# Logits three steps ahead of the weighted sums, the exponential one step behind its input, and masked places written by memsets

## The chip, the cores and the metric

The kernel runs on one core of a Trainium2 chip. The core has a matmul engine (PE, with PEld for the loading of weights), three engines for elementwise work (DVE, ACT and POOL) and SP, which here only issues DMAs. ACT issues some DMAs too. Each engine works through its own queue of instructions in order. An instruction waits for what it needs, and everything behind it on that engine waits with it. The metric is the device time of one execution in microseconds; of several runs the median is given.

## The reference

The input x has 2048 rows of 512 numbers. Each row is normalised, and the result xn goes two ways: into an attention over a sliding, dilated window (path A), and into a gated MLP with a product over all rows (path B).

```python
xn = _layernorm(x)
# A: H = 32 heads of Dh = 16, W = 8 taps at a distance of dil = 2 rows
q, k, v = split(xn @ wqkv)
idx = pos[:, None] - off[None, :]          # pos - 0, 2, .. 14
logits = einsum("bhsd,bhswd->bhsw", q, k[idx]) * Dh ** -0.5
logits = where(idx >= 0, logits, -1e9)
s = einsum("bhsw,bhswd->bhsd", softmax(logits), v[idx]) @ wo
# B
z = gelu(xn @ w_in)                        # 512 -> 2 * 896
z1, z2 = z[..., :896], layernorm(z[..., 896:])
g = w_sp @ z2 + b_sp                       # 2048 x 2048 by 2048 x 896
out = x + s * silu((z1 * g) @ w_out)
```

Masked are only the first 14 rows of the sequence, for which a tap would lie before row 0.

## The kernel before, in words

**PE's work.** All large products are done in float32 by three products each: a weight and its partner are split into a high and a low part, and high by high, high by low and low by high are added up in a PSUM bank. The high part is a copy on ACT (L186), the low part a subtraction on DVE (L187), both from a raw tile that a DMA has brought in (L163, four raw buffers). Every weight that PE uses thus passes through SP, ACT and DVE. PE's program in order: the products for q, k and v (L374 to L376), z1 (L640 to L660), z2 (L670 to L735), the product over rows with w_sp (L764: first block rows c = 2 and 3, into banks called g; then block products by a scheme with fewer products, into banks called p and q, whose weights are sums of blocks of w_sp, kept in sums_d, and whose partners are sums of blocks of z2, kept in t_d), w_out (L979 to L981) and wo.

**z2.** A tile z2_j of 128 rows stands in two banks, z2_j_0 with 512 columns and z2_j_1 with 384. Gelu on ACT reads each into the SBUF tile zt_j (L678), and the bank is then free for another product; the last four z2 banks become four of the banks g. Statistics are made on DVE (L687, aggregated by L688), a reciprocal root on POOL (L689 to L692), the normalisation on ACT (L696), then the split into BIG (L186, L187). Sums of two tiles' parts (L709, DVE) are stored to t_d from ACT's queue (L715).

**Attention.** q, k and v are written to DRAM (qkv_d) and read back by units: 8 groups of heads by two halves of the 16 rows that each of the 128 partitions holds, 16 units in all, and each unit in two steps of NJ = 4 rows. A partition holds 16 consecutive rows of the sequence, so the 14 masked ones are all on partition 0. For a step, the scores (L521) multiply eight shifted rows of k by q, the heads (L528) sum over 16 columns into lg. When a unit has all its logits, `shifted` adds the mask (L542), takes the maximum (L546), subtracts it (L547) and lets ACT take the exponential (L550). Then `normed` divides by the sum (L555, L556, L557), `weighted` multiplies v by lg (L563), a first fold (L573) adds four taps to four on POOL (for the last steps on DVE), and `finish` folds on (L578, L579), transposes (L586) and stores (L589, to o_d). Each of k, q, v, pr and pv has one buffer, lg has two. The loads of k and q (L501, L502) and of v (L510) are issued by SP.

**What sets the order.** Except for the exponential, the first fold and the DMAs, attention's instructions are chained in the order in which they are written (`line`). All of attention has a low priority (the heads a high one), and a scheduler weaves this chain into the work that feeds PE, on each engine's queue, ahead of the run, by its own costs. The program that comes out is fixed. Moving attention's steps against each other therefore also moves what stands between them on DVE, ACT, POOL and SP.

Of the kernel before, what the change touches and what calls it, by code (L numbers as in the profile page):

```python
# [11 lines left out]
F32 = mybir.dt.float32  # L12
F32R = mybir.dt.float32r
AF = mybir.ActivationFunctionType
ALU = mybir.AluOpType
AX = mybir.AxisListType

P = 128
# [3 lines left out]
H, DH, W, DIL = 32, 16, 8, 2  # L22
NT = S // P
# [11 lines left out]
CS = D // NSUB  # L35
Q = 32
HS = CS // DH
NBLK = GC // CS
HALO = (W - 1) * DIL
NJ = 4  # L40
PAD = 16
NH = NT // 2
# [3 lines left out]
MASKED = -1e9 * float(DH) ** 0.5  # L46
# [6 lines left out]
NOSYNC = mybir.DependencyInfo(mybir.DependencyClass.NoSync, mybir.DependencyReason.DATA)  # L53
# [4 lines left out]
def kernel(  # L58
# [13 lines left out]
    nc = tc.nc  # L72
# [14 lines left out]
    const = ctx.enter_context(tc.tile_pool(name="const", bufs=1, side="right"))  # L87
    opened = tc.tile_pool(name="tmp", bufs=1, side="right")
    tmp = opened.__enter__()
# [19 lines left out]
    nc.vector.memset(mvx, 0.0)  # L109
    mvz = const.tile([P, NT, 2], F32, name="mvz")  # L110
    nmz = const.tile([P, NT], F32, name="nmz")
    mask = const.tile([P, W, NT], F32, name="mask")

    BIG = whole.tile([P, NT * 2 * FH + 32], F32R, name="BIG")[:, 32:]

# [260 lines left out]
            nc.tensor.matmul(pq, xl[:, k], wh, start=False, stop=k == KB - 1)  # L376
        return pq

    zpad = const.tile([PAD, CS], F32, name="zpad")
    nc.vector.memset(zpad, 0.0)  # L380
    nc.vector.memset(mask, 0.0)
    for w in range(1, W):
        nc.vector.memset(mask[0:1, W - 1 - w, : DIL * w], MASKED)

    def weights(g, raw=[None] * KB):
        return [prep(wqkv[:, g, k, :], GC, f"wqkv_{g}_{k}", raw=raw[k]) for k in range(KB)]
# [91 lines left out]
    ap_ = ctx.enter_context(tc.tile_pool(name="att", bufs=1))  # L478

    def attention():  # L480
        saved = tc.cur_priority
        tc.cur_priority = LOW
        units = [(sub, h) for sub in range(NSUB) for h in range(2)]
        qs, ks, vs, lgs = {}, {}, {}, {}
        last = []

        def line(ins):
            if last:
                tc.add_manual_dep(ins.ins, last[-1].ins.name, NOSYNC, reason="attention in order")
            last.append(ins)  # L490
            return ins
# [26 lines left out]
        def scores(u, j0):  # L518
            pr = ap_.tile([P, W, NJ * CS], F32, tag="pr", name=f"pr_{u}_{j0}")
            qb = qs[u][:, j0 : j0 + NJ, :].rearrange("p j c -> p (j c)")  # L520
            line(nc.vector.tensor_tensor(  # L521
                pr, taps(ks[u], j0), qb.unsqueeze(1).to_broadcast([P, W, NJ * CS]), op=ALU.mult
            ))
            return pr

        def heads(u, j0, pr):
            tc.cur_priority = 0
            line(nc.vector.tensor_reduce(  # L528
                lgs[u][:, :, j0 * HS : (j0 + NJ) * HS],
                pr.rearrange("p w (i d) -> p w i d", d=DH),  # L530
                axis=AX.X,
                op=ALU.add,
            ))
            tc.cur_priority = LOW

        def shifted(u):
            sub, h = units[u]
            n = NH * HS
            lg = lgs[u]
            lgv = lg.rearrange("p w (j h) -> p w j h", h=HS)  # L540
            mk = mask[:, :, h * NH : (h + 1) * NH]
            line(nc.vector.tensor_tensor(  # L542
                lgv, lgv, mk.unsqueeze(3).to_broadcast([P, W, NH, HS]), op=ALU.add
            ))
            mx = ap_.tile([P, n], F32, tag="mx", name=f"mx_{u}")
            line(nc.vector.tensor_reduce(mx, lg.rearrange("p w i -> p i w"), axis=AX.X, op=ALU.max))  # L546
            line(nc.vector.tensor_tensor(  # L547
                lg, lg, mx.unsqueeze(1).to_broadcast([P, W, n]), op=ALU.subtract
            ))
            nc.scalar.activation(lg, lg, AF.Exp, scale=float(DH) ** -0.5)  # L550

        def normed(u):
            n, lg = NH * HS, lgs[u]
# [17 lines left out]
        def first_fold(part, eng):  # L571
            pv = part[2]
            eng.tensor_tensor(pv[:, 0:4], pv[:, 0:4], pv[:, 4:8], op=ALU.add)  # L573
# [18 lines left out]

        def start(u):
            load_qk(u)
            lgs[u] = ap_.tile([P, W, NH * HS], F32, tag="lg", name=f"lg_{u}", bufs=2)

        steps = [(u, j0) for u in range(len(units)) for j0 in range(0, NH, NJ)]
        ahead = NH // NJ
        start(0)
        for j0 in range(0, NH, NJ):  # L600
            heads(0, j0, scores(0, j0))
        shifted(0)
        part = None
        for i, (u, j0) in enumerate(steps):
            coming = steps[i + ahead] if i + ahead < len(steps) else None
            if coming:
                if not coming[1]:
                    start(coming[0])
                pr = scores(*coming)
            if part:  # L610
                finish(part)
            if not j0:
                load_v(u)
                normed(u)
            part = weighted(u, j0)
            if coming:
                heads(*coming, pr)
            first_fold(part, nc.gpsimd if coming else nc.vector)
            if coming and coming[1] + NJ == NH:
                shifted(coming[0])  # L620
        finish(part)
# [164 lines left out]
    for c in (2, 3):  # L786
        for n, js in enumerate(order):
            w = spatial.get((c, js)) or spatial_block(c, js)
# [122 lines left out]
    with urgent(400):  # L911
        for f in range(3):
# [5 lines left out]
        steps=([], [T2[0]], [T2[1]], [T2[2]]),  # L918
# [4 lines left out]
        steps=(  # L923
            [T2[3], later(upper_first, 0)],
            [T3[0], later(upper_first, 2)],
            [T3[1], later(late, 2, 0, 2)],
            [T3[2], later(late, 2, 2, 2)],
        ),
# [87 lines left out]
    for i in range(0, NT, 2):  # L1016
        j0 = rows_of[i]
# [67 lines left out]
```

## Time and profile before

| | |
|---|---|
| median of 3 runs | 720.46 us (719.02 to 720.86) |
| the profiled execution | 719.89 us, its span 718.1 us |
| PE busy | 704.5 us, 98% |
| DVE busy | 591.3 us, 82% |
| ACT busy | 266.2 us, 37% |
| POOL busy | 114.5 us, 16% |
| mean granted clock of PE | 0.995 |

An engine's busy time is time in which one of its instructions runs. In the timelines, a row gives the start in us from the span's start, the duration, engine, line, operation and out<-in (names without their buffer's number), and in brackets how long the engine had been idle before it and what ended the wait. In the list of waits the numbers are the total in us, how many waits, and the longest. In the table by stretches each row is a stretch, its length, and then busy time (and instructions) of PE, PEld, DVE, ACT and POOL, the granted clock, the share of the DMA engines and GB/s. The lines of the changed kernel are numbered a little differently (L186 and L187 stay near, L678 becomes L681, L696 becomes L699, L951 becomes L954).

### The profile page before, as it was taken

What the parts mean: (1) busy time and instruction counts of PE and PEld (TensorE: products, weight loads), DVE (VectorE), ACT (ScalarE), POOL (GpSimd) and SP (SyncE); (2) the same over time, 40 slices, a digit from 0 to 9 for tenths busy, and PEclk for the clock granted to TensorE, in tenths of its full rate; (3) what the DMA queues carried; (4) which work ended last, traced back from release to release, by engine and by line L of the source; (5) the groups of instructions that cost most, each with busy time, mean ns of one, the idle gap of its engine ahead of it and who ended that gap; (6) DMA issues with size and microseconds to landing.
All of it is one profiled execution on the core that took longest, in us unless ns stands there. A gap on an engine that the chain in (4) does not pass through costs nothing.

```text
span 718.1 us, 9084 instructions
## 1 busy us (share of the span) xinstructions
PE 704.5 (98%) x3152; PEld 587.3 (82%) x3152; DVE 591.3 (82%) x788; ACT 266.2 (37%) x417; POOL 114.5 (16%) x111
## 2 busy tenths in 40 slices
PE   8999999999999999799999999999998999999998
PEld 7888888888888899688888888888886888888886
DVE  6773579998999899999899999899999999330374
ACT  4343332333334566751213111325455443141520
POOL 3100011221121545421021121120110110000000
PEclk9999999999999999999999999999999999999999
DMA  8777677685987224289977843868778483264685
GB/s 281 242 198 221 181 259 215 206 244 208 332 284 260 87 73 147 98 269 342 362 238 251 293 150 108 286 208 303 248 250 294 129 285 133 103 190 176 234 285 199
DMA packets 100110, 159.29 MB, mean 222 GB/s; under 512 B 9056, under 2 KB 51296, under 8 KB 100064
## 3 DMA queue, kind: packets, MB, share of 16 engines
q1 hardware_dynamic: 61424, 116.11, 49.6%
q10 hardware_dynamic: 38640, 42.60, 17.2%
q8 instruction: 24, 0.39, 0.2%
q14 instruction: 22, 0.18, 0.1%
HBM read 107.74 MB, written 50.94 MB: 221 GB/s over the span
## 4 chain that ended last, share of the span: by engine, by line
PE 55%; DVE 21%; DMA 13%; issue 6%; ACT 2%; POOL 2%; SPq 1%; DVEq 0%; ACTq 0%
PE g L764 21%; PE q L764 5%; PE b L980 4%; PE b L979 4%; PE b L981 4%; DVE lg L528 3%; PE p L764 3%; DMA sb<-in_w_sp 3%; DVE pr L521 3%; DVE pv L563 3%; PE qkv L374 2%; PE qkv L376 2%; PE qkv L375 2%; PE s L980 2%; PE s L979 2%
## 5 line engine op out<-in xcount | busy, mean ns | idle before, releaser
L573 POOL TENSOR_TENSOR pv<-pv 128x1024 f32<-128x1024 f32 x30 | 72.2, 2407 | 393.3 <-DVE pv L563 393.3
L521 DVE TENSOR_TENSOR pr<-k,q 128x2048 f32<-128x2048 f32 x32 | 73.2, 2289 | 6.2 <-DMA q<-qkv_d 4.4
L563 DVE TENSOR_TENSOR pv<-v,lg 128x2048 f32<-128x2048 f32 x32 | 73.2, 2288 | 0.5
L528 DVE TENSOR_REDUCE lg<-pr 128x128 f32<-128x2048 f32 x32 | 72.9, 2278 | 0.0
L394 ACT ACTIVATE stage<-qkv 128x512 f32<-128x512 f32 x36 | 21.4, 594 | 41.8 <-PE qkv L376 41.7
L990 ACT ACTIVATE bt<-b 128x512 f32<-128x512 f32 x16 | 9.3, 597 | 45.7 <-PE b L981 45.7
L677 PE MATMUL z<-w_0h,BIG 128*128 128x512 f32 x64 | 25.0, 391 | 0.0
L676 PE MATMUL z<-w_0l,BIG 128*128 128x512 f32 x64 | 25.0, 391 | 0.0
L1034 DVE TENSOR_TENSOR sg<-s,sg 128x512 f32<-128x512 f32 (+1 forms) x17 | 11.2, 660 | 16.7 <-PE s L981 16.7
L675 PE MATMUL z<-w_0h,BIG 128*128 128x512 f32 x64 | 24.9, 389 | 0.0
L696 ACT ACTIVATE zt<-zt,nmz,mvz 128x896 f32<-128x896 f32 x16 | 17.8, 1133 | 16.1 <-POOL nmz L692 16.1
L187 DVE TENSOR_TENSOR o_1l<-ol,o_1h 128x512 fp32r<-128x512 f32 x3 | 2.1, 690 | 26.1 <-ACT o_1h L186 26.1
L270 DVE TENSOR_TENSOR xT<-xT,mr 128x512 f32<-128x512 f32 x20 | 13.8, 688 | 10.5 <-DMA mr<-mv_d 6.2
L578 DVE TENSOR_TENSOR pv<-pv 128x512 f32<-128x512 f32 x32 | 21.9, 683 | 0.1
L677 PE MATMUL z<-w_1h,BIG 128*128 128x384 f32 x64 | 21.5, 336 | 0.0
L675 PE MATMUL z<-w_1h,BIG 128*128 128x384 f32 x64 | 21.5, 335 | 0.0
L676 PE MATMUL z<-w_1l,BIG 128*128 128x384 f32 x64 | 21.4, 335 | 0.0
L687 DVE BATCH_NORM_STATS2 zst<-zt 128x6 f32<-128x448 f32 x32 | 19.3, 613 | 2.1 <-ACT zt L678 2.1
L186 ACT ACTIVATE BIG<-tr 128x768 fp32r<-128x768 f32 x16 | 13.3, 839 | 15.9 <-DMA tr<-t_d 15.9
L187 DVE TENSOR_TENSOR BIG<-zt,BIG 128x896 fp32r<-128x896 f32 x16 | 17.1, 1081 | 1.3 <-ACT BIG L186 1.3
L656 ACT ACTIVATE z1t<-z 128x512 f32<-128x512 f32 x21 | 12.4, 592 | 15.3 <-PE z L649 4.5
L636 DVE TENSOR_TENSOR sb<-sa,sb 128x512 f32<-128x512 f32 x16 | 11.5, 721 | 7.3 <-DMA sb<-in_w_sp 6.3
(545 smaller groups left out, 2204.3 us busy)
## 6 DMA issues: line engine op xcount, KB each, us to landing
qkv_d<-stage ACTq DMA_DIRECT2D x24, 512.0 KB
k<-qkv_d SPq DMA_DIRECT2D x16, 704.0 KB
v<-qkv_d SPq DMA_DIRECT2D x16, 704.0 KB
z_d<-z1t ACTq DMA_DIRECT2D x14, 512.0 KB
t_d<-zt ACTq DMA_DIRECT2D x16, 384.0 KB
zl<-z_d SPq DMA_DIRECT2D x12, 512.0 KB
tr<-t_d SPq DMA_DIRECT2D x16, 384.0 KB
x<-in_x SPq DMA_DIRECT2D x16, 256.0 KB
```

Of the source, the lines that this page charges most:

```text
L521: line(nc.vector.tensor_tensor(pr, taps(ks[u], j0), qb.unsqueeze(1).to_broadcast([P, W, NJ * CS]), op=ALU.mult))
L528: line(nc.vector.tensor_reduce(lgs[u][:, :, j0 * HS : (j0 + NJ) * HS], pr.rearrange("p w (i d) -> p w i d", d=DH), axis=AX.X, op=ALU.add,))
L563: line(nc.vector.tensor_tensor(pv.rearrange("p w (i d) -> p w i d", d=DH), taps(vs[u], j0).rearrange("p w (i d) -> p w i d", d=DH), lgs[u] ...
L573: eng.tensor_tensor(pv[:, 0:4], pv[:, 0:4], pv[:, 4:8], op=ALU.add)
L578: line(nc.vector.tensor_tensor(pr[:, 0:2], pr[:, 0:2], pr[:, 2:4], op=ALU.add))
L675: nc.tensor.matmul(pz, xh[:, k], wh, start=k == 0, stop=False)
L676: nc.tensor.matmul(pz, xh[:, k], wl, start=False, stop=False)
L677: nc.tensor.matmul(pz, xl[:, k], wh, start=False, stop=k == KB - 1)
L764: nc.tensor.matmul(pg, z[a], w[b], start=start and i == 0, stop=stop and i == 2, skip_group_check=seeded)
L979: nc.tensor.matmul(pp[:, cols], hi, wh, start=k == 0, stop=False)
L980: nc.tensor.matmul(pp[:, cols], hi, wl, start=False, stop=False)
L981: nc.tensor.matmul(pp[:, cols], lo, wh, start=False, stop=k == n - 1)
```

## The change

The tile `mask` and its additions are gone. Instead each unit overwrites the masked places of its logits, on partition 0 alone, with memsets: seven for the first half of the rows and three for the second, since further taps reach no further there. Logits run three steps ahead of the weighted sums rather than two, for which lg has three buffers. The maximum and its subtraction follow as soon as a unit's logits are complete, one step earlier against the weighted sums than before. The exponential leaves `shifted` and is issued after the second step of the unit before, chained behind that place. The fold goes to DVE when nothing is coming any more, which is now the last three steps, not the last two. `zpad`, a tile of zeros for the start, is taken from another pool.

```diff
-    mask = const.tile([P, W, NT], F32, name="mask")
...
-    zpad = const.tile([PAD, CS], F32, name="zpad")
+    zpad = tmp.tile([PAD, CS], F32, tag="zpad", name="zpad", bufs=1)
     nc.vector.memset(zpad, 0.0)
-    nc.vector.memset(mask, 0.0)
-    for w in range(1, W):
-        nc.vector.memset(mask[0:1, W - 1 - w, : DIL * w], MASKED)
...
-            lgv = lg.rearrange("p w (j h) -> p w j h", h=HS)
-            mk = mask[:, :, h * NH : (h + 1) * NH]
-            line(nc.vector.tensor_tensor(
-                lgv, lgv, mk.unsqueeze(3).to_broadcast([P, W, NH, HS]), op=ALU.add
-            ))
+            for w in range(1, W):
+                if DIL * w > h * NH:
+                    front = min(DIL * w - h * NH, NH) * HS
+                    line(nc.vector.memset(lg[0:1, W - 1 - w, :front], MASKED))
...
-            nc.scalar.activation(lg, lg, AF.Exp, scale=float(DH) ** -0.5)
+
+        def exponential(u):
+            ins = nc.scalar.activation(lgs[u], lgs[u], AF.Exp, scale=float(DH) ** -0.5)
+            tc.add_manual_dep(ins.ins, last[-1].ins.name, NOSYNC, reason="well behind the shift")
...
-            lgs[u] = ap_.tile([P, W, NH * HS], F32, tag="lg", name=f"lg_{u}", bufs=2)
+            lgs[u] = ap_.tile([P, W, NH * HS], F32, tag="lg", name=f"lg_{u}", bufs=3)
...
-        ahead = NH // NJ
-        start(0)
-        for j0 in range(0, NH, NJ):
-            heads(0, j0, scores(0, j0))
-        shifted(0)
+        ahead = NH // NJ + 1
+        for step in steps[:ahead]:
+            if not step[1]:
+                start(step[0])
+            heads(*step, scores(*step))
+            if step[1] + NJ == NH:
+                shifted(step[0])
+        exponential(0)
...
             first_fold(part, nc.gpsimd if coming else nc.vector)
+            if j0 + NJ == NH and u + 1 < len(units):
+                exponential(u + 1)
             if coming and coming[1] + NJ == NH:
                 shifted(coming[0])
```

How this moves instructions is shown at three places. A row has the line, the operation and out<-in; the number behind a name tells tiles of one name apart. First, ACT's queue at the end of the z2 stage: lg_7 is the logits of unit 7, zt_5, zt_7, zt_13, zt_14 and zt_15 are tiles of z2, wsp_2_8 and so on are weights of the product over rows. Before:

```order
L678 ACTIVATE zt_14_2896<-z2_14_1_2939 128x384
L550 ACT_TABLE_LOAD
L550 ACTIVATE lg_7_1438<-lg_7_1438 128x256
L696 ACTIVATE zt_5_2809<-zt_5_2809,nmz_95,mvz_94 128x896
L696 ACTIVATE zt_13_2810<-zt_13_2810,nmz_95,mvz_94 128x896
L186 ACTIVATE BIG_97<-zt_5_2809 128x7x128
L186 ACTIVATE BIG_97<-zt_13_2810 128x7x128
L186 ACTIVATE wsp_2_8h_3013<-wsp_2_8r_3011 128x512
L715 DMA t_d_80<-zt_4_2723 256x1x384
L186 ACTIVATE wsp_2_1h_3176<-wsp_2_1r_3174 128x512
L186 ACTIVATE wsp_2_9h_3203<-wsp_2_9r_3201 128x512
L678 ACT_TABLE_LOAD
L678 ACTIVATE zt_7_2981<-z2_7_0_2983 128x512
```

And now:

```order
L547 ACTIVATE lg_7_1447<-lg_7_1447 128x256
L681 ACT_TABLE_LOAD
L681 ACTIVATE zt_14_2951<-z2_14_0_2966 128x512
L699 ACTIVATE zt_5_2864<-zt_5_2864,nmz_95,mvz_94 128x896
L185 ACTIVATE BIG_96<-zt_5_2864 128x7x128
L718 DMA t_d_80<-zt_3_2692 256x1x384
L681 ACTIVATE zt_6_2950<-z2_6_1_2980 128x384
L681 ACTIVATE zt_14_2951<-z2_14_1_2994 128x384
L185 ACTIVATE wsp_2_8h_3068<-wsp_2_8r_3066 128x512
L185 ACTIVATE wsp_2_1h_3231<-wsp_2_1r_3229 128x512
L699 ACTIVATE zt_13_2865<-zt_13_2865,nmz_95,mvz_94 128x896
L681 ACTIVATE zt_7_3036<-z2_7_0_3038 128x512
```

The exponential of unit 7 and its table loads went ahead of zt_14, the normalisation and split of zt_5 ahead of zt_14's second half, and the split of zt_13 behind zt_7's first gelu. Second, the same queue at the switch from one block product (banks q5) to the next (weights q3): va and vb are copies of banks q that PE then fills again, tr_10_2 is a pair of blocks loaded from t_d. Before:

```order
L186 ACTIVATE BIG_97<-tr_10_2_4963 128x2x3x128
L186 ACTIVATE q3_3h_4941<-q3_3r_4939 128x512
L186 ACTIVATE q3_4h_4975<-q3_4r_4973 128x512
L186 ACTIVATE q3_5h_4981<-q3_5r_4979 128x512
L951 ACTIVATE va_4748<-q5_0_4753 128x512
L951 ACTIVATE vb_4749<-q5_1_4754 128x512
```

And now:

```order
L185 ACTIVATE q3_3h_4996<-q3_3r_4994 128x512
L185 ACTIVATE BIG_96<-tr_10_2_5018 128x2x3x128
L185 ACTIVATE q3_4h_5030<-q3_4r_5028 128x512
L954 ACTIVATE va_4803<-q5_0_4808 128x512
L954 ACTIVATE vb_4804<-q5_1_4809 128x512
L185 ACTIVATE q3_5h_5036<-q3_5r_5034 128x512
```

The copies va and vb stand ahead of q3_5h now. Third, SP's queue there, with the loads of these weights and blocks; zl_1_4 is a block of z1. Before:

```order
L821 DMA tr_10_0_4919<-t_d_80 128x2x384
L163 DMA q3_1r_4895<-sums_d_79 128x512
L163 DMA q3_2r_4933<-sums_d_79 128x512
L773 DMA zl_1_4_4923<-z1_d_77 128x2x512
L821 DMA tr_10_2_4963<-t_d_80 128x2x384
L163 DMA q3_3r_4939<-sums_d_79 128x512
```

And now:

```order
L824 DMA tr_10_0_4974<-t_d_80 128x2x384
L587 DMA o_d_82<-tt_13_0_1836 32x2x128 x4
L506 DMA v_7_0_1857<-qkv_d_75 128x1408
L162 DMA q3_2r_4988<-sums_d_79 128x512
L776 DMA zl_1_4_4978<-z1_d_77 128x2x512
L162 DMA q3_3r_4994<-sums_d_79 128x512
L824 DMA tr_10_2_5018<-t_d_80 128x2x384
```

The stores of tt_13_0 (unit 13) and the load of v for unit 14, which stood well ahead of this place, come between the two tr loads.

## The prediction

> **What bounds the kernel now.** I read the page first, then the list of waits of the matmul engine (PE), the table by stretches, the chain that ended last, and the timelines of the two stretches the first views point to.
>
> ```profile
> span 718.1 us, 9084 instructions
> PE 704.5 (98%) x3152; PEld 587.3 (82%) x3152; DVE 591.3 (82%) x788; ACT 266.2 (37%) x417; POOL 114.5 (16%) x111
> ```
>
> PE is busy for 704.5 of 718.1 us, so all the idle time that any change of order can win back is 13.6 us, and part of that is the start and the end. Work taken off DVE wins nothing by itself: it has to shorten a wait of PE. The list of PE's waits has two that count, and no other of 1.5 us or more:
>
> ```profile
> PE g L764 <- ACT zt L678: 4.6, 1, 4.6
> PE q L764 <- ACT va L951: 3.2, 1, 3.2
> ```
>
> The table by stretches (PE, PEld, DVE, ACT, POOL, then granted clock, DMA share, GB/s) shows what surrounds them:
>
> ```profile
> 297.00:302.00 5.00, 0.43 (x3) 0.01 (x1) 4.94 (x11) 4.97 (x8) 3.28 (x7) 1.00 0.30 84
> 302.00:306.00 4.00, 4.00 (x10) 2.90 (x11) 4.00 (x9) 4.00 (x7) 0.91 (x2) 0.57 0.88 298
> 545.00:550.00 5.00, 5.00 (x24) 4.13 (x22) 4.80 (x9) 2.24 (x5) 0.00 (x0) 1.00 0.95 302
> 555.00:559.00 4.00, 4.00 (x12) 3.10 (x12) 4.00 (x3) 2.52 (x5) 1.16 (x1) 0.57 0.53 158
> ```
>
> After each idle stretch the clock is granted at 0.57 for 4 us: 10 and 12 matmuls, where the five us before 550 at full clock hold 24 (so 4 us some 19). Each stall thus costs about 7 to 9 matmuls more, at 5/24 = 0.21 us some 1.5 to 2 us. Both stalls with their slow clock are worth about 4.6 + 2 + 3.2 + 1.5 = 11 us; 719.89 - 11 = 709 is the most that this change can reach.
>
> First stall, by the chain that ended last (and, in the last two rows, DVE's and POOL's timeline):
>
> ```profile
> 291.57 2.46 POOL mvz L691
> 295.67 1.12 ACT zt L696
> 296.79 0.56 ACT BIG L186
> 297.53 0.93 ACT BIG L186
> 300.05 1.28 ACT L678
> 301.34 0.61 ACT zt L678
> 301.99 151.61 PE g L764 x660
> ...
> 290.92 0.19 DVE L688 BATCH_NORM_AGGREGATE mvz<-zst 128x2 f32<-128x12 f32 x1
> 295.19 0.19 POOL L692 TENSOR_TENSOR nmz<-nmz,mvz 128x1 f32<-128x1 f32 x1
> ```
>
> PE's next product needs the bank from which the gelu at 301.34 reads zt_7. That gelu stands in ACT's queue behind two normalisations, two BIG splits, three weight splits and a table load, and the normalisations wait on POOL, which got its statistics from DVE at 290.92 and was through at 295.4. Between the end of the first stall and 453 PE runs without a gap. Second stall, in ACT's timeline and PE's:
>
> ```profile
> 549.70 0.85 ACT L186 ACTIVATE BIG<-tr 128x768 fp32r<-128x768 f32 x1 [2.76 <-DMA tr<-t_d]
> 550.45 0.62 ACT L186 ACTIVATE q_3h<-q_3r 128x512 fp32r<-128x512 f32 x1
> 551.01 0.63 ACT L186 ACTIVATE q_4h<-q_4r 128x512 fp32r<-128x512 f32 x1
> 553.54 0.63 ACT L186 ACTIVATE q_5h<-q_5r 128x512 fp32r<-128x512 f32 x1 [1.89 <-DMA q_5r<-sums_d]
> 554.07 0.58 ACT L951 ACTIVATE va<-q 128x512 f32<-128x512 f32 x1
> 554.71 0.50 PE L764 MATMUL q<-q_0h,BIG 128*128 128x512 f32 x1 [3.19 <-ACT va L951]
> ```
>
> The copy va, for which PE waits, needs nothing that comes late; it stands behind q_5h, whose raw weight lands at 553.5.
>
> **The change, part by part.** *Masks.* The adds and the start's memsets go, 80 small memsets come (7 and 3 per pair of units, 8 pairs):
>
> ```profile
> L542 DVE TENSOR_TENSOR lg<-lg,mask x16: 403/418/605, 91.3 to 590.5; 128x256 f32<-128x256 f32 x16
> 1.20 0.16 DVE L383 MEMSET mask<- 1x2 f32 x7
> L383 DVE MEMSET mask<- x7: 60/65/70, 1.2 to 1.3; 1x2 f32 x1, 1x4 f32 x1, 1x6 f32 x1, 1x8 f32 x1
> L573 DVE TENSOR_TENSOR pv<-pv x2: 1224/1224/1225, 608.8 to 614.0; 128x1024 f32<-128x1024 f32 x2
> L187 DVE TENSOR_TENSOR o_1l<-ol,o_1h 128x512 fp32r<-128x512 f32 x3 | 2.1, 690 | 26.1 <-ACT o_1h L186 26.1
> ```
>
> Out: 16 x 0.42 = 6.7 us. In: seven memsets in a row fill 0.16 us, 0.023 each, so 80 x 0.023 = 1.8 us; at their own 0.065 us each, 5.2 us. I take 1.8, because they stand in rows as those seven do, and keep 5.2. DVE gains 4.9 us (1.5 at the other end). The Trainium skill (VectorE: DVE Perf Modes, The DRAIN you can't avoid) speaks against this edit: each DVE operation pays for emptying its pipe before the next starts, so fewer operations are better. By it the memsets would cost nearer the 5.2 us; the trace, with seven in 0.16 us, does not agree for these. One first fold moves from POOL to DVE (1.22) near the end of attention; DVE then waits 26.1 us for o_1h, which covers it, and without that cover it costs 1.2. The third lg buffer and the moved zpad cost no time.
>
> *Order of the logits and the exponential.* No work is added, but whatever shares a queue is moved. At the first stall the exponential of unit 7 with its two table loads goes from behind zt_14's second half to ahead of its first half; normalisation and split of zt_5 are done early; and zt_13's split goes behind zt_7. Left ahead of zt_7 is: the last statistics of zt_13 (290.92; about 1.5 us of work further back in the new row of DVE, so 292.4), POOL's chain (4.5 us in the trace, for two tiles at once, of which I take 3 for one), the normalisation 1.12, zt_7's gelu 0.61: 292.4 + 3 + 1.1 + 0.6 = 297.1, just when PE arrives. But the second gelu of zt_7, next in PE's order, now follows two weight splits and a BIG split (0.6 + 0.6 + 0.9 + 0.6 = 2.7, 299.8), and PE reaches it at 297.9. So of 4.6 us idle some 2 stay, too short perhaps for the slow clock: PE leads by 3 to 5 us from there (2.6 of the wait, and 2 of the slow clock). The Trainium skill (ScalarE: Activation LUTs, What ACT_TABLE_LOAD costs) adds a drain of about 1.4 us to each load; by it the exponential's move would free 2.8 us more. Here the gelu at 301.34 starts right behind the load of 1.28 at 300.05, so the trace does not agree.
>
> To carry a lead of 3 to 5 us to 551, PE needs its weights as much earlier. Tight is the stretch 507 to 548, where DVE ends a weight's low part shortly before PE uses it, as at its end:
>
> ```profile
> 545.24 0.69 DVE L187 TENSOR_TENSOR q_7l<-q_7r,q_7h 128x512 fp32r<-128x512 f32 x1
> 547.96 0.39 PE L764 MATMUL q<-q_7h,BIG 128*128 128x512 f32 x1
> ```
>
> The low part is ready at 545.9 and used at 548.2, 2.3 us later. In the new row of DVE some 2 to 8 us less attention work stands in front of these splits (scores, folds and sums that now come behind them; for this one 3.8). So the lead should hold.
>
> *The second stall is where it is cashed.* va now stands ahead of q_5h, but still behind q_4h, and that behind the tr load that landed at 549.70. So va runs at 551.64 instead of 554.07: 2.4 us sooner, however early PE arrives. From there PE has no wait of 1.5 us to the end (the list above), and I let it run as before. Whether tr lands as before is open, because of SP's row:
>
> ```profile
> 527.81 0.34 SPq L510 DMA_DIRECT2D v<-qkv_d  x1
> 545.36 0.37 SPq L821 DMA_DIRECT2D tr<-t_d  x1
> 546.56 0.33 SPq L163 DMA_DIRECT2D q_4r<-sums_d  x1
> v<-qkv_d SPq DMA_DIRECT2D x16, 704.0 KB
> ```
>
> The v load of unit 14 and four stores of tt_13_0 now stand between tr_10_0 and tr_10_2, instead of before q_3r of the product ahead. At 302 GB/s its 704 KB are 2.4 us of a stretch that is already 0.95 full. Against that, DVE releases the buffers of these loads 0.2 to 4 us earlier. I take the two as cancelling (0), with +2.4 and -3 as ends.
>
> *The sum.* 719.89 (the profiled run) - 2.4 = 717.5; the first stall's gain is not added, as it is spent waiting at the second. The median shown, 720.46, is 0.6 above the profiled run, which I leave out. About 0.3% (2.2 us) is what can be told from no change here.
>
> **Rivals.** *More of it:* DVE's 2 to 8 us less work brings tr and q_4r 2 to 3 us sooner, and va with them: 719.89 - 2.4 - 3 = 714.5, and at most 709 if both stalls go. For it: in the chain the loads here follow DVE's splits. Against: DMA share 0.95. *Given back:* v's 2.4 us of transfer push tr and va back as far as the queue move brought them forward: 719.9. For it: the same share; against: the transfers around 530 get free instead.
>
> *Slower:* v, with a single buffer, becomes a wait. Its load starts when the last weighted product of a unit ends, and has to land before the next one. The shift of the coming unit (mask 0.42, max, subtract) no longer lies in that time; at least one score, one reduction and one fold do:
>
> ```profile
> L521 DVE TENSOR_TENSOR pr<-k,q 128x2048 f32<-128x2048 f32 x32 | 73.2, 2289 | 6.2 <-DMA q<-qkv_d 4.4
> L528 DVE TENSOR_REDUCE lg<-pr 128x128 f32<-128x2048 f32 x32 | 72.9, 2278 | 0.0
> L578 DVE TENSOR_TENSOR pv<-pv 128x512 f32<-128x512 f32 x32 | 21.9, 683 | 0.1
> 75.34 4.73 DMA k<-qkv_d
> 97.16 2.29 DVE L521 TENSOR_TENSOR pr<-k,q 128x2048 f32<-128x2048 f32 x1 [4.35 <-DMA q<-qkv_d]
> 90.23 0.58 SPq L502 DMA_DIRECT2D q<-qkv_d  x1
> ```
>
> That cover is 2.29 + 2.28 + 0.68 = 5.25 us and two us of short steps. The k load took 4.73, and q, issued right behind a k, came 6.9 us after its issue. Should v need 8, DVE loses about 1 us at each of the 14 units up to 551, and once that sum exceeds the 4 to 8 us by which its work moved ahead, the splits of 507 to 545 come late: 14 - 8 = 6 us more at PE, 726. For it: DVE is busy for 4.80 of the 5 us before 550. Against: v has never been waited for so far.
>
> **How the numbers follow.** The forecast, 717.5 with its own range of 715.5 to 719, gets 0.38; more of it 0.17; given back 0.20 (718.5 to 721.5); slower 0.25 (722 to 728; into it goes a like delay from the statistics of z2 late in DVE's row). Faster than 718.3: most of the first, all of the second, 0.49. Within 0.3%: the rest of the first and half or more of the third, 0.21. Slower than 722.6: 0.30. For 8 in 10 the range leaves out a tenth at either end: 712 to 725.
>
> **What would show it.** The wait on zt down from 4.6 to about 2 us and no 0.57 behind it; the wait on va now longer (5 us or more, as PE comes early), but ending near 552, with 0.57 after it; PE without a gap from there. DVE's busy time near 587. Wrong I am if a new line of over 2 us stands among PE's waits, if DVE waits for v, or if va ends as late as 554 behind a later tr.

## The result, and the profile after

The changed kernel takes 708.59 us (median of four runs, 707.93 to 709.92), the kernel before beside it 719.74 us (718.97 to 720.86). The ratio is 0.9846 with a 95% interval of 0.9824 to 0.9868: 1.5% faster, 11 us. The forecast was 717.5 with a range of 712 to 725, so the direction was right and the size was not: the time is below the range, at the ceiling of 709 that the prediction had worked out for the case that both stalls go.

The page of the changed kernel, its list of PE's waits, and its table by stretches (columns as before):

```profile
span 706.6 us, 9137 instructions
PE 700.8 (99%) x3152; PEld 585.6 (83%) x3152; DVE 586.4 (83%) x845; ACT 268.3 (38%) x417; POOL 112.6 (16%) x110
...
PE warm L278 <- POOL ident masks.py:199: 1.3, 1, 1.3
PE xt L217 <- DVE mvx L202: 0.4, 1, 0.4
...
297.00:302.00 5.00, 5.00 (x24) 4.14 (x23) 5.00 (x12) 1.31 (x2) 3.90 (x8) 1.00 0.91 312
302.00:306.00 4.00, 4.00 (x19) 3.34 (x18) 3.97 (x9) 2.85 (x5) 1.14 (x4) 1.00 0.84 322
545.00:550.00 5.00, 5.00 (x24) 4.14 (x23) 4.96 (x10) 2.91 (x5) 0.00 (x0) 1.00 0.90 288
555.00:559.00 4.00, 4.00 (x19) 3.31 (x18) 4.00 (x2) 1.35 (x3) 1.80 (x1) 1.00 0.80 278
```

Both waits are gone from the list; what is left belongs to the start. The stretches that held 3 matmuls in five us, and then 10 and 12 in four us at a clock of 0.57, now hold 24 and 19 at full clock. The 11.5 us between the two spans (718.1 and 706.6) are the two waits, 4.6 + 3.2, and 3.7 us less of busy time on PE (700.8 against 704.5), since no matmuls run at the slow clock any more.

ACT's timeline at the first place and at the second, and DVE's memsets:

```profile
291.14 1.14 ACT L699 ACTIVATE zt<-zt,nmz,mvz 128x896 f32<-128x896 f32 x1 [1.18 <-POOL nmz L695]
292.19 0.58 ACT L681 ACTIVATE zt<-z 128x512 f32<-128x512 f32 x1
294.55 0.48 ACT L681 ACTIVATE zt<-z 128x384 f32<-128x384 f32 x1
...
541.35 0.85 ACT L185 ACTIVATE BIG<-tr 128x768 fp32r<-128x768 f32 x1 [0.26 <-DMA tr<-t_d]
542.10 0.62 ACT L185 ACTIVATE q_4h<-q_4r 128x512 fp32r<-128x512 f32 x1
542.62 0.57 ACT L954 ACTIVATE va<-q 128x512 f32<-128x512 f32 x1
544.29 0.63 ACT L185 ACTIVATE q_5h<-q_5r 128x512 fp32r<-128x512 f32 x1
...
L539 DVE MEMSET lg<- x80: 65/78/85, 91.5 to 564.0; 1x32 f32 x32, 1x8 f32 x16, 1x16 f32 x16, 1x24 f32 x16
511.71 0.20 DVE L539 MEMSET lg<- 1x24 f32 x4
511.84 0.64 DVE L876 TENSOR_TENSOR yb<-q,yb 128x512 f32<-128x512 f32 x1
```

zt_7's first gelu runs at 292.19 instead of 301.34 and its second at 294.55, both before PE needs them. The copy va runs at 542.62 instead of 554.07. That is 11.5 us sooner, where the prediction had 2.4, and the blocks tr ahead of it land 8.4 us sooner, where it had "as before". PE's last matmul ahead of va's place, in the kernel before, and then that matmul and the next one now:

```profile
551.13 0.39 PE L764 MATMUL q<-q_7h,BIG 128*128 128x512 f32 x1
```

```profile
544.73 0.39 PE L767 MATMUL q<-q_7h,BIG 128*128 128x512 f32 x1
544.95 0.39 PE L767 MATMUL q<-q_0h,BIG 128*128 128x512 f32 x1
```

PE comes to this place 6.4 us sooner, which is the first stall with its slow clock, and leaves it 9.8 us sooner (554.71 before), which adds 3.4 us for the second wait. The 1.7 us that are left of the 11.5 fall behind it, where the slow clock was.

### The profile page after: what moved, and what is told of

It reads as the page before. It is cut to its first block, busy times and chain, and to the rows that moved or that the text cites. A ratio compares the mean times of both kernels' runs of the same rounds, so it can differ in the third digit from the quotient of the medians.

```text
span 706.6 us, 9137 instructions
## 1 busy us (share of the span) xinstructions
PE 700.8 (99%) x3152; PEld 585.6 (83%) x3152; DVE 586.4 (83%) x845; ACT 268.3 (38%) x417; POOL 112.6 (16%) x110
## 4 chain that ended last, share of the span: by engine, by line
PE 98%; DMA 1%; DVE 1%; SPq 0%; issue 0%
PE g L767 22%; PE q L767 12%; PE p L767 6%; PE qkv L373 6%; PE qkv L375 6%; PE qkv L374 6%; PE z L680 4%; PE z L679 4%; PE z L678 4%; PE z L652 4%; PE b L983 4%; PE z L650 4%; PE b L984 4%; PE b L982 4%; PE z L651 4%; PE s L983 2%
## 5 line engine op out<-in xcount | busy, mean ns | idle before, releaser
L571 POOL TENSOR_TENSOR pv<-pv 128x1024 f32<-128x1024 f32 x29 | 69.8, 2406 | 377.1 <-DVE pv L561 377.0
L375 PE MATMUL qkv<-wqkv_0h,BIG 128*128 128x512 f32 x43 | 16.7, 389 | 0.0
L373 PE MATMUL qkv<-wqkv_1h,BIG 128*128 128x512 f32 x43 | 16.7, 389 | 0.0
```

What stands on the lines that cost most here:

```text
L373: nc.tensor.matmul(pq, xh[:, k], wh, start=k == 0, stop=False)
```

## The experiments

Nearly every edit here makes the scheduler weave attention into the rest anew: of the 788 places of DVE's row in the kernel before, little more than half stand in the same order in the changed one. The first runs therefore take the change apart; the next ones set single places by hand, which leaves the order of DVE's row nearly as it was. Nine of the fourteen runs ended outside every range that was given for them, so the theories in the expectations are tried out here rather than confirmed.

### The parts alone

Only the masks:

```diff
-            line(nc.vector.tensor_tensor(
-                lgv, lgv, mk.unsqueeze(3).to_broadcast([P, W, NH, HS]), op=ALU.add
-            ))
+            for w in range(1, W):
+                if DIL * w > h * NH:
+                    front = min(DIL * w - h * NH, NH) * HS
+                    line(nc.vector.memset(lg[0:1, W - 1 - w, :front], MASKED))
...
-        ahead = NH // NJ + 1
+        ahead = NH // NJ
```

> Only the masks: the memsets replace the mask tile's adds; logits two steps ahead, two lg buffers and the exponential inside the shift stay as before. Theory W (PE's two stalls go as soon as DVE gives zt_13's last statistics 3 to 4 us sooner, whatever edit does that): DVE's new row has 2.8 us less work ahead of those statistics and ACT's has no weight split ahead of zt_7, so the wait on zt falls from 4.6 to about 1 us, the wait on va from 3.2 to 0 to 2 us, and the time is 709 to 713. Theory O (the logits three steps ahead carry it): the waits stay, 718 to 721.

Measured: 714.54 us, ratio 0.9935 (0.9915 to 0.9954). Only the order, with the mask tile kept:

```diff
-            lgs[u] = ap_.tile([P, W, NH * HS], F32, tag="lg", name=f"lg_{u}", bufs=3)
...
         def heads(u, j0, pr):
+            if not j0:
+                lgs[u] = ap_.tile([P, W, NH * HS], F32, tag="lg", name=f"lg_{u}", bufs=2)
...
-            for w in range(1, W):
-                if DIL * w > h * NH:
-                    front = min(DIL * w - h * NH, NH) * HS
-                    line(nc.vector.memset(lg[0:1, W - 1 - w, :front], MASKED))
+            line(nc.vector.tensor_tensor(
+                lgv, lgv, mk.unsqueeze(3).to_broadcast([P, W, NH, HS]), op=ALU.add
+            ))
```

> Only the order: logits three steps ahead and the exponential on its own, but the mask tile and its 16 adds stay; as three lg buffers do not fit beside the mask, lg has two, given out at the first sum of a unit. DVE's busy time stays near 591. Theory W: the row has 0.9 us less work ahead of zt_13's statistics; if idle time of DVE before 290 goes too (9.2 us between 100 and 290 in the kernel before, 5.1 in the changed one), the time is 708 to 712. Theory M (the 4.9 us that the masks take off DVE carry it): 717 to 721.

Measured: 712.33 us, ratio 0.9914 (0.9886 to 0.9942). Each part alone gives about half, 4.7 and 6.2 us by the ratios; neither "the masks carry it" nor "the order carries it" holds. What of PE's waits stays, in the kernel with the masks and in that with the order:

```profile
PE g L759 <- ACT g L778: 1.9, 1, 1.9
PE g L759 <- ACT zt L673: 1.6, 2, 1.1
```

```profile
PE q L773 <- ACT va L960: 2.5, 1, 2.5
PE g L773 <- ACT g L792: 1.3, 1, 1.3
```

In both, the first stall is gone or small. The kernel with the order still waits 2.5 us at va, and the waits on g stand at a place where the kernel before has none. The exponential's place by itself:

```diff
-        def exponential(u):
-            ins = nc.scalar.activation(lgs[u], lgs[u], AF.Exp, scale=float(DH) ** -0.5)
-            tc.add_manual_dep(ins.ins, last[-1].ins.name, NOSYNC, reason="well behind the shift")
+            nc.scalar.activation(lg, lg, AF.Exp, scale=float(DH) ** -0.5)
```

> The changed kernel, with the exponential back inside the shift; the rows of PE, DVE, POOL and SP are the same as in the changed kernel, ACT's differs in 26 of 504 places. Theory W: no difference, 707.5 to 709.5. Theory E (the exponential's later place keeps ACT free at the right moments): a wait of 1 us or more on ACT comes back at PE, 710 to 716.

Measured: 709.36 us, ratio 0.9878 (0.9831 to 0.9924), which cannot be told from the changed kernel's. PE waits 0.3 us on zt. In this run zt_13's last statistics come at 291.2, as late as in the kernel before (290.9), and zt_7's gelu still starts at 295.0 instead of 301.3: with what stands in ACT's queue now, the first stall goes even with these statistics as late as before.

### The two places in ACT's queue, set by hand in the kernel before

```diff
+                if name == "q3" and s == 5:
+                    behind.append(copies[1])
...
         first_ = pin(nc.scalar.activation(hi, src, AF.Copy))
+        if behind:
+            tc.add_manual_dep(first_.ins, behind[0].ins.name, NOSYNC, reason="after the copy")
```

> The kernel before, with one edit: ACT's copies va and vb are put ahead of the split of q3_5h. Nothing else moves but that. The prediction's second term alone: the wait on va falls from 3.2 to about 0.8 us, and with it 2.4 us of the time: 717 to 718. Theory W: the same, since DVE and the loads are as late as before; the wait on zt stays at 4.6 and the time does not fall under 716.

Measured: 715.54 us, ratio 0.9965 (0.9943 to 0.9987), 2.5 us against the kernel before of the same runs (the medians differ by 3.0). The prediction's second term, 2.4 us, was about right for what it described, the copy's place. The wait at va is gone altogether, where 0.8 us was expected, and the wait on zt stands at 4.2 us.

```diff
+        if (j, h) in [(7, 0)]:
+            gelus.append(ins)
...
+        behind.extend(gelus if j in (5, 13) else [])
         split(zh, zl, blocks(zt, FB))
+        behind.clear()
...
+        behind.extend(gelus if c == 2 and js in (1, 8, 9) else [])
```

> The kernel before, with zt_7's first gelu put ahead of the splits of zt_5, zt_13 and of the weights wsp_2_8, wsp_2_1 and wsp_2_9 on ACT; attention, masks and the copies va and vb stay. The wait on zt falls from 4.6 to 1 to 2 us. The prediction's step (the lead is spent at the second stall, whose end is set by loads that do not care when PE comes): the wait on va grows to 6 us, the time stays at 717.5 to 720. Theory F (buffers and loads follow PE and DVE, so that the loads come as much earlier as PE leads): the wait on va stays near 3 and the time falls by 3 to 5 us, to 713.5 to 716.

Measured: 722.73 us, ratio 1.0047 (1.0016 to 1.0079), a little slower. The gelu comes 3.8 us sooner and the wait on zt shrinks as meant, but other waits follow, and the one at va stays:

```profile
PE q L777 <- ACT va L964: 3.1, 1, 3.1
PE p L777 <- ACT p L796: 1.8, 1, 1.8
PE g L777 <- ACT zt L684: 1.5, 2, 1.0
...
PE g L777 <- DVE wsp_8l L191: 0.9, 1, 0.9
PE g L777 <- ACT g L796: 0.9, 1, 0.9
```

DVE's split wsp_8l starts at 299.6 (300.1 before) and tr_10_2 is split at 550.7 (549.7 before): DVE and the loads are as late as ever, PE catches up with them a few us further on, and va ends where it did. So the lead is lost again, as the prediction's step "the second stall is where it is cashed" has it, but not there: the wait at va is 3.1 us, as before, and not the 6 that were expected. It is lost at the waits in between, on zt, wsp_8l, g and p.

> Both edits of ACT's queue in the kernel before: zt_7's first gelu ahead of the five splits, and va and vb ahead of q3_5h. Attention and masks stay. Theory Q (the two places in ACT's queue are all of the gain): both waits under 1.5 us and no stretch of slow clock, 708 to 711. The prediction's steps (first gain spent at the second stall, second gain 2.4): 715 to 717. If DVE's pace is what carries it (theory W): a wait of 2 us or more stays or appears elsewhere, 712 to 716.

Measured: 719.63 us, ratio 1.0007 (0.9979 to 1.0034). Both places together bring nothing, less than the copies alone. So setting these two places is not enough for the gain. The two waits themselves did not go: 2.7 us on zt and 2.0 at va are left in the profiled execution, which at 722.82 us is the slowest of the ten.

### The room in the DMA engines

```diff
+            if u == 14:
+                cp = nc.sync.dma_start(spare_d, w_sp[0, :2])
+                tc.add_manual_dep(cp.ins, ld.ins.name, NOSYNC, reason="behind the load")
```

> The changed kernel with a copy of 0.5 MB from DRAM to DRAM (1 MB of traffic, about 3.3 us at 302 GB/s) issued by SP right behind the load of v for unit 14; the rows of all other engines are the same, word for word. If the DMA engines bound the stretch before 551, as the prediction's end of +2.4 had it, the blocks tr_10_2 land 3 us later and PE waits 2 to 3 us on va: 711 to 712.5. If the changed kernel has room there: no difference, 707.5 to 709.5.

> The same with a copy of 1 MB (2 MB of traffic, about 6.6 us at 302 GB/s); 20 of 845 places of DVE's row differ from the changed kernel's. DMA-bound: PE waits 5 to 6 us on va and loses 1.5 us more by the slow clock, 714 to 716. With room of some 3 us: 710 to 712. With more room than 6 us: 707.5 to 709.5.

Measured: 708.83 us, ratio 0.986 (0.9818 to 0.9902), and with 1 MB 708.64 us, 0.9856 (0.9814 to 0.9898). Neither costs time that can be seen, but the loads do feel the copies: from SP's issue of tr_10_2 to its split on ACT it takes 5.2 us in the changed kernel (536.17 to 541.35), 5.7 with 0.5 MB and 6.6 with 1 MB. PE has room for that. In the changed kernel va ends at 543.2 and PE goes on at 544.95; with 1 MB hardly any of this room is left, though va stands ahead of q3_4h too in that run:

```profile
544.11 0.58 ACT L958 ACTIVATE va<-q 128x512 f32<-128x512 f32 x1
544.80 0.44 PE L771 MATMUL q<-q_0h,BIG 128*128 128x512 f32 x1
```

So 1 MB more delays the blocks by 1.5 us, not by 6.6, and the changed kernel can just bear it. For v's 704 KB that makes about 1 us (an estimate from these 1.5), less than the prediction's end of +2.4. Nor were the 302 GB/s behind that figure a ceiling: with the 1 MB copy the table by stretches has

```profile
533.00:536.00 3.00, 3.00 (x15) 2.48 (x14) 3.00 (x5) 2.26 (x4) 0.47 (x1) 1.00 1.62 559
```

### DVE's position

Two numbers can be read from the trace for each kernel: when DVE starts q3_1l (one of the last weights ahead of va), and how long it was busy until then; the rest is idle time. The table by stretches, from 0 to that start, gives it: the kernel before, the changed one, and the kernel with two buffers (below).

```profile
0.00:547.60 547.60, 540.76 (x2428) 451.92 (x2429) 490.18 (x648) 209.60 (x328) 109.72 (x109) 1.00 0.70 229
```

```profile
0.00:540.30 540.30, 538.12 (x2424) 450.53 (x2425) 488.80 (x703) 211.38 (x328) 110.23 (x109) 1.00 0.72 234
```

```profile
0.00:550.20 550.20, 541.34 (x2415) 451.92 (x2416) 492.71 (x700) 209.40 (x328) 108.95 (x109) 0.99 0.70 228
```

DVE's busy time differs by 1.4 us between before and after (490.2 and 488.8), its idle time by 5.9 us (57.4 and 51.5). Over the whole run DVE is busy 4.9 us less in the changed kernel, but the scheduler fills that room with other attention work ahead of q3_1l. Four more runs vary DVE's work, each with a new weave:

```diff
+            if (u, j0) in [(2, 4)]:
+                line(nc.vector.tensor_tensor(
+                    pr, taps(ks[u], j0), qb.unsqueeze(1).to_broadcast([P, W, NJ * CS]), op=ALU.mult
+                ))
```

> The changed kernel with one score product (2.28 us of DVE) done twice, in the second step of unit 2. Theory D (the end follows the copy va, whose time is DVE's work ahead of q3_1l plus DVE's idle time up to there, and a constant of some 162.5 us from va to the end): the new row has 489.6 us of work ahead of q3_1l against 488.8, so with the changed kernel's idle time, 51.5, it stands at 541 and PE does not wait: 707.5 to 710. Theory P (each new weave is a new lot): idle time may be as high as 57, q3_1l at 547, and the time 712 to 716.

Measured: 708.57 us, ratio 0.9835 (0.9806 to 0.9864).

```diff
+            if (u, j0) in [(2, 4), (4, 4)]:
+                return prs[-1]
             pr = ap_.tile([P, W, NJ * CS], F32, tag="pr", name=f"pr_{u}_{j0}")
+            prs.append(pr)
```

> The kernel before without the second score product of units 2 and 4 (the heads of those steps sum the first step's products again): 4.6 us less work on DVE, masks, order and ACT's queue at va of the old kind (va behind q3_5h). Theory D: 486.5 us of work ahead of q3_1l against 490.2; with the idle time of before, 57.4, q3_1l stands at 544 and va some 6 us later: 714 to 717. If work on DVE does not matter: 718.5 to 721.

Measured: 709.21 us, ratio 0.9844 (0.9815 to 0.9874): more than expected, all of the gain, with the order and the masks of the kernel before (but with two score products left out). Both numbers that theory D added up were off: the work ahead of q3_1l is 488.1 us, not 486.5, and the idle time fell from 57.4 to 49.8.

```diff
+            line(nc.vector.tensor_tensor(lg, lg, lg, op=ALU.max))
             mx = ap_.tile([P, n], F32, tag="mx", name=f"mx_{u}")
```

> The changed kernel with 16 more operations on DVE, of the size of the mask's adds (the larger of lg and lg, 128 x 256, after the memsets): the 6.7 us are given back, the order stays of the new kind. va stands behind q3_5h. Theory D: 488.9 us of work ahead of q3_1l; idle time 51.5 to 57 gives 540 to 546, va some 4 to 6 us later: 709 to 715. Theory M (the masks' 4.9 us are the gain): 713 to 718.

Measured: 708.33 us, ratio 0.9832 (0.9798 to 0.9866). With the masks' work given back to DVE (595.3 us busy, more than before the change) the time is that of the changed kernel.

```diff
-            lgs[u] = ap_.tile([P, W, NH * HS], F32, tag="lg", name=f"lg_{u}", bufs=3)
...
         def heads(u, j0, pr):
+            if not j0:
+                lgs[u] = ap_.tile([P, W, NH * HS], F32, tag="lg", name=f"lg_{u}", bufs=2)
```

> The changed kernel with two lg buffers instead of three, a buffer being given out at a unit's first sum. Theory D: 485.1 us of work ahead of q3_1l (488.8 in the changed kernel); with idle time of 51.5 to 57 q3_1l stands at 537 to 542, and though va stands behind q3_5h here, PE waits for it 2 us at most: 707.5 to 712. Theory B (the third buffer is what lets attention run ahead and DVE idle less): idle time of 57 or more, 713 to 718.

Measured: 720.22 us, ratio 1.0013 (0.9986 to 1.004): the whole gain is gone, outside the ranges of both theories. This kernel is "order only" with the memsets in place of the mask's adds; the memsets alone brought 4.7 us, the order alone 6.2, and both together bring nothing. The parts do not add up, and the third buffer cannot be called the cause, as "order only" gains with two buffers as well.

In one table, sorted by the start of va (times in us, of the profiled executions; the last column is the median of the runs; "elsewhere" are PE's other waits after the first 100 us, those of 0.3 us or more):

| kernel | DVE busy up to q3_1l | idle up to q3_1l | q3_1l starts | va starts | PE waits at va | elsewhere | span | median |
|---|---|---|---|---|---|---|---|---|
| changed | 488.8 | 51.5 | 540.3 | 542.6 | 0 | 0 | 706.6 | 708.6 |
| one score more | 489.4 | 50.4 | 539.8 | 542.7 | 0 | 0 | 706.9 | 708.6 |
| two scores less | 488.1 | 49.8 | 537.9 | 543.4 | 0 | 0 | 706.6 | 709.2 |
| sixteen more | 488.9 | 50.6 | 539.5 | 543.5 | 0 | 0 | 707.1 | 708.3 |
| exponential at once | 488.0 | 54.2 | 542.2 | 544.0 | 0 | 0.3 | 707.1 | 709.4 |
| copy of 1 MB | 488.8 | 52.1 | 540.9 | 544.1 | 0 | 0 | 706.7 | 708.6 |
| copy of 0.5 MB | 487.9 | 53.5 | 541.4 | 544.2 | 0 | 0 | 707.1 | 708.8 |
| sums later, va first (below) | 488.7 | 52.1 | 540.8 | 546.2 | 2.1 | 0 | 710.2 | 718.5 |
| order only | 489.0 | 54.1 | 543.1 | 548.4 | 2.5 | 1.3 | 710.9 | 712.3 |
| masks only | 488.9 | 56.5 | 545.4 | 551.0 | 0.4 | 3.5 | 713.4 | 714.5 |
| va ahead | 490.2 | 56.1 | 546.3 | 551.0 | 0 | 4.2 | 713.9 | 715.5 |
| sums later (below) | 488.6 | 57.2 | 545.8 | 552.1 | 4.7 | 1.8 | 717.0 | 717.8 |
| before | 490.2 | 57.4 | 547.6 | 554.1 | 3.2 | 4.6 | 718.1 | 720.5 |
| gelu first | 490.5 | 58.2 | 548.7 | 554.5 | 3.1 | 5.1 | 719.7 | 722.7 |
| two buffers | 492.7 | 57.5 | 550.2 | 557.1 | 0.7 | 7.0 | 719.5 | 720.2 |
| gelu and va first | 490.3 | 63.7 | 554.0 | 558.6 | 2.0 | 7.3 | 721.0 | 719.6 |

Busy time hardly differs, idle time does, and va and the span move together: from the start of va to the end it is 162.4 to 165.2 us in every row. That alone does not make va the cause, since va copies a bank that PE must have filled first, so a PE that was held up earlier makes va late too. In "va ahead" PE does not wait at va at all, in "masks only" and "two buffers" hardly; their time is lost at other waits. What the table shows is that the kernels whose PE hardly waits have 49.8 to 54.2 us of idle time on DVE, and the others 52.1 to 63.7. Each row is one execution, and kernels whose PE waits spread by several us from one execution to the next.

Does DVE idle because PE is late, or the other way round? The stretch ahead of the first stall answers a part of it (the kernel before, then the changed one):

```profile
100.00:290.00 190.00, 190.00 (x877) 162.13 (x876) 180.84 (x214) 79.52 (x119) 54.66 (x54) 1.00 0.61 203
```

```profile
100.00:290.00 190.00, 190.00 (x877) 162.15 (x876) 184.53 (x250) 86.95 (x127) 56.41 (x61) 1.00 0.64 204
```

PE runs without a gap in both, and DVE idles 9.2 us before and 5.5 now. These 3.7 us are no result of PE's waits. Another 4.0 lie between 310 and 490 us (9.2 and 5.2 us idle), behind the first stall, where a late PE may be part of the reason; but "sums later" below has no first stall and idles 8.9 us there. (In the first 100 us the changed kernel idles 1.2 us more.)

### What DVE waits for

The largest of DVE's waits between 100 and 545 us in the kernel before, the changed one, and the one with two buffers:

```profile
DVE sb L636 <- DMA sb<-in_w_sp: 6.3, 4, 2.4
```

```profile
DVE sb L639 <- issue: 2.1, 1, 2.1
```

```profile
DVE sb L640 <- DMA sb<-in_w_sp: 9.7, 4, 3.8
```

These are the adds of the block sums, which stand in DVE's row before their loads have landed. In the changed kernel more attention work stands ahead of them. To see whether these waits alone carry it, the first adds of four block sums were moved back in the kernel before:

```diff
+            if n_ == 0 and i in behind_:
+                tc.add_manual_dep(ins.ins, chain[behind_[i]].ins.name, NOSYNC, reason="sums later")
...
+    behind_ = {0: 69, 1: 87, 5: 152, 6: 159}
```

> The kernel before, in which the first add of four block sums (numbers 0, 1, 5 and 6, those for whose loads DVE waits) comes two to three attention steps later in DVE's row; masks, lead of the logits, exponential and the queue at va stay. Work ahead of q3_1l: 489.9 us, as before. Theory D: DVE's waits for the loads sb (6.3 us in the kernel before) fall under 3, its idle time up to q3_1l from 57.4 to 52 to 54, q3_1l from 547.6 to 542 to 545, and the time by 3 to 5 us, to 713.5 to 716; the wait on va of the old kind stays. If these waits are only a sign and not the cause (other waits take their place): idle time stays at 56 to 58 and the time at 717 to 721.

> The same, and va and vb ahead of q3_5h on ACT. Theory D: both edits together reach what the changed kernel reaches, less the wait on zt, which PE can now work off before va: 708 to 712. If DVE's waits are not the cause: as with va and vb alone, 714.5 to 717.

Measured: 717.81 us, ratio 0.9981 (0.995 to 1.0012), and with the copies first 718.51 us, 0.9977 (0.9946 to 1.0009): no gain. Up to zt_13's statistics the edit did what it should: they come at 284.4 instead of 290.9, and the wait on zt is gone. Then DVE loses it again. Its waits from 294 to 490 with the sums moved:

```profile
DVE sb L639 <- DMA sb<-in_w_sp: 5.5, 3, 3.0
DVE wsp_4l L187 <- ACT wsp_4h L186: 3.6, 1, 3.6
DVE zl L815 <- DMA zl<-z_d: 1.3, 1, 1.3
DVE BIG L187 <- ACT BIG L186: 1.3, 1, 1.3
```

and the same stretch in the table, of this kernel and of the changed one:

```profile
294.00:490.00 196.00, 194.22 (x856) 160.21 (x855) 183.45 (x229) 53.12 (x87) 33.83 (x24) 1.00 0.74 247
```

```profile
294.00:490.00 196.00, 196.00 (x867) 162.40 (x866) 190.64 (x265) 56.09 (x89) 37.92 (x28) 1.00 0.78 263
```

DVE idles 12.6 us of these 196 here, 5.4 in the changed kernel. PE, now early, runs into va (a wait of 4.7 us), and the end is where it was. The one profiled execution of the second kernel, 711.98 us, is the best of its ten runs; in it DVE stood at q3_1l with 52.1 us of idle time, and PE still waited 2.1 us at va, which started at 546.2. Its other runs, 715 to 720 us, have no trace.

So this does not decide whether the waits for the block sums are the cause. The edit moved them rather than taking them away: from 100 to 545 us they come to 6.4 us in "sums later", as against 6.3 before. That they are not all of it is shown by "two scores less", which has 4.6 us of them and all of the gain. Why just the weaves with the lead and the third buffer (and that with two scores less) leave DVE so little idle time is not settled. No run beats the changed kernel: those with 708.3 to 709.4 cannot be told from it, and PE's 700.8 us of work leave little.

## Why the prediction was wrong

**What bounds the kernel** was right: two waits of PE with their stretches of slow clock are all that an order can win, and the ceiling of 709 was met within half a us.

**The masks' price.** The term of 1.8 us for the memsets was too small. Taken for their line alone, the table by stretches has 4.06 us of DVE's time for the 80 memsets, and 7.21 for the 16 adds, where the prediction had 6.7; the saving is 3.2 us rather than 4.9. Where four stand in a row they fill 0.13 us up to the next start (511.71 to 511.84), 0.033 each against the 0.023 that were taken. That DVE's busy time came out at 586.4, "near 587", is therefore no proof of this price. The Trainium skill (VectorE: DVE Perf Modes, The DRAIN you can't avoid) has the next operation start only when the pipe is empty, and adds that one that is not held starts earlier; at 0.065 to 0.085 us each, four of these memsets in 0.13 us overlap, so the plain rule does not hold for them. That DVE's busy time by itself wins nothing held: with all of it given back (sixteen more), the time is the same.

**The first stall.** The term "some 2 stay" was mis-sized; 0 stayed. POOL's chain took 2.7 us from the statistics (288.46 in DVE's row) to the normalisation at 291.14, not 3, and the statistics came four us earlier than the 292.4 that I had from counting work in front of them. The order on ACT was the part that I had right: in the run with the exponential at once, with the statistics at 291.2, PE waits only 0.3 us.

**The step that failed** is "the second stall is where it is cashed", and in it "I take the two as cancelling (0)". There, 2.4 us for the transfer of v stood against 0.2 to 4 us less work on DVE, so that the blocks tr would land at 549.70 as before and PE would spend its lead waiting for va. They landed at 541.35. The count of work was not far off (1.4 us less up to q3_1l), but a position in a row is work plus idle time, and the idle time fell by 5.9 us, a term that the prediction left out; the list of DVE's waits, with 6.3 us on sb, was at hand. With the loads 8.4 us sooner, va came 11.5 us sooner: 8.4 from the loads, about 2.5 from its place ahead of q_5h (2.5 us measured for that place alone, 2.4 forecast), and the rest from the order of the splits around it. So the 6.4 us by which PE came to this place sooner were kept, and the wait there went as well. Why DVE idled less stays open. The other half of the step, that a lead of PE alone is lost again when the loads are as late as before, is borne out: "gelu first" loses it at four waits on the way, "sums later" at va (4.7 us against 3.2) and at p.

**The rivals.** "More of it" was the case that came, with its bound of 709; it got 0.17, and its own price, 714.5, rested on 2 to 3 us for the loads. "Given back" did not come: the blocks landed 8.4 us sooner with v's load between them, and the copy of 1 MB delays them by only 1.5 us. "Slower", by a wait for v, did not come: v is in no list of DVE's waits of 0.5 us or more in the changed kernel.

## What to carry to other kernels

When a scheduler weaves one chain of work into another, count two things for the engine that is woven: the work ahead of the instruction that matters, and the time the engine stands idle before it. The first stays nearly constant here (488 to 493 us under all edits), so the difference is in the second (50 to 64 us), and it cannot be read from a count of work. Before costing a stall that is won early as "lost again at the next one", look at what feeds the next one: if it hangs on an engine that the change also moves, it may come sooner too.

## What the runs showed of the hardware that I had not expected

The length of a wait does not by itself say whether the slow clock follows. A wait of 2.5 us at va left the clock at 1.00 (order only, first row), and so did one of 2.5 us on zt (two buffers). One of 4.7 us was followed by four us at 0.50 (sums later, second row), in which 9 matmuls ran where "order only" runs 17. But one of 2.65 us on zt was followed by six us at 0.50 as well (gelu and va first, third row), and one of 1.9 us on g by four us at 0.63 (masks only, from 377.05). All waits of 3.1 us or more, six in these traces, had the slow clock behind them:

```profile
549.00:553.00 4.00, 3.92 (x17) 3.25 (x18) 4.00 (x3) 2.35 (x6) 2.07 (x1) 1.00 0.91 262
```

```profile
552.70:556.70 4.00, 3.99 (x9) 3.14 (x10) 4.00 (x6) 2.70 (x5) 0.00 (x0) 0.50 0.58 178
```

```profile
302.06:308.06 6.00, 5.98 (x13) 4.31 (x14) 6.00 (x11) 6.00 (x10) 1.85 (x6) 0.50 0.69 226
```

The Trainium skill (TensorE: Matmul & The Clock Gate, What's actually happening) puts the border at an idle window of about 3.4 us; the first two rows agree with it, the waits of 2.65 and 1.9 us do not, and what brought the slow clock there stays open.

The runs' spread differs too. The kernel before took 715.3 to 724.5 us over all its runs beside these experiments, the changed kernel 707.9 to 709.9 over four, and the other kernels at the floor 708.0 to 709.9, but for one run of 714.5 with the exponential at once. It would fit that a kernel whose PE never waits does not notice when a load lands a little later, as the copies showed for 1.5 us; no run varied the loads of the kernel before.
